# The last block's output projection made twice: three split products, and whole-precision products beside them

## The chip, the cores and the metric

The kernel runs on one core of one Trainium2 chip. The metric is the device time of one execution in microseconds (us). A core has a matrix engine (TensorE, PE in the profile, its weight loads PEld), a vector engine (VectorE, DVE), a scalar engine (ScalarE, ACT), a general engine (GpSimd, POOL) and a sync engine (SyncE, SP), which here issues nearly all DMA transfers. Each engine works through its own list of instructions in order and waits on semaphores for the others.

## What is computed

A transformer block with modulation by a condition, on 2048 rows of 512 numbers; 32 heads of 16 numbers share one key and one value head. All inputs and outputs are 32-bit floats.

```python
sa, ca, ga, sb, cb, gb = six rows of 512 from silu(c) @ w_mod
h = layernorm(x) * (1 + ca) + sa
x = x + ga * (softmax(q k' / 4) v) @ wo          # q = h @ wq, k = h @ wk, v = h @ wv
h = layernorm(x) * (1 + cb) + sb
x = x + gb * (gelu(h @ w1 + b1) @ w2 + b2)
```

The change concerns the third line for the last 256 rows alone: the output projection `@ wo`, with `ga` already multiplied into its weights.

## The kernel before, in words

**Blocks and units.** The rows go in eight blocks of 256. A block has eight attention units of four heads; the units' score products, exponentials and value products fill most of the run. What follows a block's attention (output projection, second layer norm, the two MLP layers) is a generator, `rest_steps` (L813), which hands out batches of matrix products. For blocks 0 to 6 they are woven between the attention of the next block. The last block (number 7, `fast=True`) has nothing left to be woven into; its products are issued whole, by `whole` (L181, products at L183), one after another at the end of the program.

**Split products.** A 32-bit operand is kept as two tiles of the type fp32r, a rounded one ("H") and the rest ("L"). A product is then three: H by H, H by L and L by H, added in PSUM. `batches` (L167) lists them. For the output projection, `out_pairs` (L858) gives the attention result `onH`, `onL` as the stationary operand (128 x 128) and the weights `woH`, `woL` as the moving one (128 x 512). There are four groups of 128 contraction rows (`KD` = 4) and two row tiles `t` of 128 rows, so 24 products for the block.

**The last block step by step.** Three of the four groups are projected early (18 products). The fourth waits for the last attention unit, whose sums are inverted (L691), go through DRAM (L694, L669) and scale the unit's result (L671); then it is split on ScalarE (L132) and VectorE (L137). During that wait the generator yields `TAIL[0]` = 4 ticks, and in each tick `tick` (L1473) issues a batch of what is left of block 6's second MLP layer (`w2ps`). Then the six products of the last group follow. For each row tile, VectorE adds x to the sum (`add_x`, L833), takes the statistics in two halves (`stats`, L840), joins them (`rstd`, L846 and L847), GpSimd takes the power -1/2 (L849), and VectorE makes the normalized rows `xh` (`xhat`, L852). Meanwhile `yield TAIL[1]` (L884, 8 ticks) lets block 6's last 24 `w2ps` products be issued. Then TensorE transposes `xh` (`turn2`, L917, with four filler products at L811, `stir`, after each row tile), ScalarE scales and shifts (L905), the result is split again, and the two MLP layers follow (`w1ps`, `w2ps`), with GELU on ScalarE and VectorE between them. At the end `store` (L1008) adds x1 to the sums (L1011) and sends 256 KB per row tile to DRAM (L1012).

**Pools and banks that matter.** The tile tag `ot` has two buffers that are used in turn; the output tiles of `store` live there, so a buffer is free again only when its transfer to DRAM has landed. `xh` has one buffer. `bank()` (L731) gives PSUM banks in a fixed rotation. SyncE's list has, shortly before the last projection, three transfers of 1024 KB each for MLP weights (L829), and then block 6's two output tiles (L1012), one whose sum is ready before the last projection, and one after block 6's last 24 products.

Of the kernel before, what the change touches and what calls it, by code (L numbers as in the profile page):

```python
# [8 lines left out]
F32 = mybir.dt.float32  # L9
F32R = mybir.dt.float32r  # L10
AF = mybir.ActivationFunctionType
ALU = mybir.AluOpType
AX = mybir.AxisListType

P = 128
# [30 lines left out]
def raw(ap):  # L46
    return ap.bitcast(F32)
# [3 lines left out]
def adaln_mqa_mlp(  # L51
# [15 lines left out]
    nc = tc.nc  # L67
    _, S, D = x.shape
# [3 lines left out]
    KD = D // P  # L72
# [18 lines left out]
    psum = ctx.enter_context(tc.tile_pool(name="psum", bufs=1, space=bass.MemoryType.PSUM))  # L91
# [49 lines left out]
    state = {"mods": False, "q": NB * KD, "busy": False, "turns": 1}  # L141
# [25 lines left out]
    def batches(ps, pairs, size, ready=lambda n: True, begin=True, end=True):  # L167

        todo = [(a, b_) for wh, wl, xh, xl in pairs for a, b_ in ((wh, xh), (wl, xh), (wh, xl))]
        last = len(todo) - 1  # L170

        ends = list(range(len(todo), 0, -size))[::-1]
        if ends[0] == 1:
            ends.pop(0)
        for begin_, end_ in zip([0] + ends, ends):
            part = range(begin_, end_)
            while not ready(part[-1] // 3):
                yield -1
            yield [(ps, *todo[n], begin and n == 0, end and n == last) for n in part]
# [544 lines left out]
    def rest(b, fast):  # L724
# [61 lines left out]
        ready = {}  # L786
        later(*((4, lambda: norm(0)) if fast else (2, fetch)))
        return rest_steps(b, fast, rp, bank, ons, ready)

    early = {}  # L790
# [22 lines left out]
    def rest_steps(b, fast, rp, bank, ons, ready):  # L813
# [3 lines left out]
        woH, woL = wts_pool["wo"]  # L817
        for hf in range(w // HQ):
# [5 lines left out]
            x1, w1ts = early[b]  # L824
            xh = rp.tile([P, 2, D], F32, name=f"xh2_{b}_{hf}", tag="xh2", bufs=1)
# [6 lines left out]
            def add_x(t, ps):  # L832
                nc.vector.tensor_tensor(out=x1[:, t, :], in0=ps, in1=x1[:, t, :], op=ALU.add)  # L833
# [5 lines left out]
            def stats(t, h):  # L839
                nc.vector.bn_stats(out=st[:, t, h, :], in_=x1[:, t, h * D // 2:(h + 1) * D // 2])  # L840
# [3 lines left out]
            def rstd(t0, t1):  # L844
                for t in range(t0, t1):
                    nc.vector.bn_aggr(out=mv[:, t, :], in_=st[:, t].rearrange("p h n -> p (h n)"))  # L846
                (nc.vector if fast else nc.gpsimd).tensor_scalar(out=ve[:, t0:t1], in0=mv[:, t0:t1, 1], scalar1=EPS,  # L847
                                                                 scalar2=0.0, op0=ALU.add, op1=ALU.add)
                nc.gpsimd.tensor_tensor(out=rs[:, t0:t1], in0=ve[:, t0:t1], in1=mhalf[:, t0:t1], op=ALU.pow)  # L849

            def xhat(t):
                (nc.vector if fast else nc.gpsimd).tensor_scalar(out=xh[:, t, :], in0=x1[:, t, :], scalar1=mv[:, t, 0:1],  # L852
                                                                 scalar2=rs[:, t:t + 1], op0=ALU.subtract, op1=ALU.mult)
# [4 lines left out]
            def out_pairs(t, gs):  # L858
                sl = slice(t * P, (t + 1) * P)
                return [(onH[:, g, sl], onL[:, g, sl], woH[:, g, :], woL[:, g, :]) for g in gs]  # L860

            pss = []
            for t in range(2):
                ps = psum.tile([P, D], F32, name=f"wops{b}_{hf}_{t}", **bank())
# [8 lines left out]
                    later(3 - 2 * t + 2 * h, lambda t=t, h=h: stats(t, h))  # L873
            if fast:
                yield TAIL[0]
                for t in range(2):
                    yield from batches(pss[t], out_pairs(t, [KD - 1]), BATCH, begin=False)
                    add_x(t, pss[t])
                    stats(t, 0)
                    stats(t, 1)  # L880
                    rstd(t, t + 1)
                for t in range(2):
                    xhat(t)
                yield TAIL[1]  # L884
# [45 lines left out]
            else:  # L930
                for dp in range(KD // 2):
                    ps = psum.tile([P, 2, HQ], F32, name=f"tp2_{b}_{hf}_{dp}", **bank())
# [55 lines left out]
            for f in range(GROUP if fast else 0, NF):  # L988
# [3 lines left out]
                ps = psum.tile([P, HQ], F32, name=f"w1ps{b}_{hf}_{f}", **bank())  # L992
# [27 lines left out]
            for t in range(2):  # L1020
                sl = slice(t * P, (t + 1) * P)
                for cols in (slice(0, D), ):
                    place = dict(tag="m", bufs=3) if b == len(blocks) - 2 and t else bank()
                    ps = psum.tile([P, D], F32, name=f"w2ps{b}_{hf}_{t}_{cols.start}", **place)
# [496 lines left out]
```

## Time and profile before

| what | us |
|---|---|
| median of 3 runs | 1563.27 (1562.41 to 1563.35) |
| the profiled execution | 1561.89 |
| its span (first to last instruction) | 1560.1 |
| PE busy | 1543.2 |
| DVE busy | 1400.8 |
| ACT busy | 1227.4 |
| POOL busy | 681.5 |
| granted TensorE clock | 1.0 in all slices |

The profile of one execution lists the instructions of each engine with start and duration. A line such as `L183 PE MATMUL w2ps<-w2H,gH 128*128 128x512` names the code line, the engine, the operation, the tile written and those read, the part of the array used (128 x 128) and the moving operand's shape. "Chain of work that ended last" is found by following back from the last instruction to whatever released each step. A busy TensorE is counted from records with modelled ends, so it says little about how closely products follow one another; their start times say more.

### The profile page before, as it was taken

The numbers are of one execution on the slowest core, as the hardware profiler recorded it, in microseconds if no ns is written. First come the engines' busy times: TensorE is split into PE (matmuls) and PEld (weight loads), VectorE is DVE, ScalarE is ACT, GpSimd is POOL, SyncE is SP. The second block draws the span as 40 slices with busy tenths as digits, with TensorE's granted clock in tenths as the row PEclk, the third lists the DMA queues.
The fourth block names the chain that finished last, engine by engine and source line by source line (L and its number), as shares of the span: only waits on it lengthen the run. The fifth ranks groups of instructions, "written<-read, shape, count | busy, mean of one in ns | idle before, by whom it ended". The sixth has DMA issues, their size and how long they took to land.

```text
span 1560.1 us, 41350 instructions
## 1 busy us (share of the span) xinstructions
PE 1543.2 (99%) x16347; PEld 955.2 (61%) x16347; DVE 1400.8 (90%) x2479; ACT 1227.4 (79%) x2392; POOL 681.5 (44%) x1194
## 2 busy tenths in 40 slices
PE   7999999999999999999999999999999999999999
PEld 4456555567655665557655675556655676556657
DVE  7999999999999999999999999999999999999725
ACT  5577778788878887788877887788877888778953
POOL 5545433867322570246522562245611474225721
PEclk9999999999999999999999999999999999999999
DMA  7225412312030211202012120302112120211241
GB/s 250 92 93 197 148 56 85 124 52 97 19 109 19 83 59 36 94 28 99 30 54 76 55 86 23 109 14 100 44 49 80 46 97 17 84 55 63 84 159 52
DMA packets 83125, 121.61 MB, mean 78 GB/s; under 512 B 19614, under 2 KB 56222, under 8 KB 82676
## 3 DMA queue, kind: packets, MB, share of 16 engines
q1 hardware_dynamic: 82916, 118.97, 22.9%
q8 instruction: 129, 2.11, 0.6%
q14 instruction: 64, 0.52, 0.1%
q10 hardware_dynamic: 16, 0.00, 0.0%
HBM read 91.13 MB, written 27.27 MB: 76 GB/s over the span
## 4 chain that ended last, share of the span: by engine, by line
PE 84%; DVE 10%; issue 3%; POOL 2%; DMA 1%; ACT 1%; SPq 0%; POOLq 0%; DVEq 0%
PE acc L633 28%; PE m L507 24%; PE e L612 15%; DVE mx L512 8%; PE w1ps L193 8%; PE w2ps L183 2%; PE w1ps L183 1%; DMA xt<-in_A_x_dram 1%; PE w2ps L193 1%; PE qps L193 1%; PE tp L193 1%; PE wops L193 1%; PE kps L162 1%; DVE st L840 1%; DVE x L833 1%
## 5 line engine op out<-in xcount | busy, mean ns | idle before, releaser
L512 DVE TENSOR_REDUCE mx<-m 128x1 f32<-128x512 f32 x2048 | 1269.3, 681 | 87.7 <-PE m L507 64.7
L616 ACT ACTIVATE p<-e 128x512 f32<-128x512 f32 x2048 | 1098.0, 598 | 254.8 <-PE e L612 106.4
L507 PE MATMUL m<-ks,qst 64*128 64x512 f32 x2048 | 832.9, 429 | 2.0 <-DVE mx L512 0.6
L612 PE MATMUL e<-qst,ks 64*128 64x512 f32 x2048 | 739.9, 413 | 0.0
L633 PE MATMUL acc<-p,va 128*32 128x256 f32 x8192 | 548.0, 385 | 0.0
L507 PEld LDWEIGHTS m<-ks,qst 64*128 64x128 f32 x2048 | 367.1, 184 | 211.6 <-DVE mx L512 174.0
L612 PEld LDWEIGHTS e<-qst,ks 64*128 64x128 f32 x2048 | 358.7, 185 | 92.3 <-ACT p L616 64.0
L633 PEld LDWEIGHTS acc<-p,va 128*32 128x32 f32 x8192 | 214.5, 109 | 213.7 <-issue 110.7
L555 POOL TENSOR_SCALAR mt<-turned 8x32 f32<-8x32 f32 x256 | 53.1, 208 | 419.5 <-DVE turned L561 407.4
L193 PE MATMUL w1ps<-h2H,w1t 64*128 64x256 f32 x1216 | 232.7, 287 | 0.0
L193 PEld LDWEIGHTS w1ps<-h2H,w1t 64*128 64x128 f32 x1216 | 183.6, 185 | 28.4 <-issue 14.4
L193 PE MATMUL w1ps<-h2L,w1t 64*128 64x256 f32 x608 | 167.0, 275 | 0.0
L193 PE MATMUL w2ps<-w2H,gH 64*128 64x512 f32 x264 | 115.9, 439 | 0.0
L193 PEld LDWEIGHTS w1ps<-h2L,w1t 64*128 64x128 f32 x608 | 112.8, 185 | 0.0
L193 PE MATMUL w2ps<-w2L,gH 64*128 64x512 f32 x264 | 103.4, 392 | 0.0
L193 PE MATMUL w2ps<-w2H,gL 64*128 64x512 f32 x264 | 103.0, 390 | 0.0
L959 POOL TENSOR_SCALAR tt<-tt 128x256 f32<-128x256 f32 x77 | 31.0, 403 | 143.1 <-ACT tt L958 109.8
L137 POOL TENSOR_TENSOR gL<-z,gH 128x256 fp32r<-128x256 f32 x77 | 56.9, 739 | 6.4
L960 POOL TENSOR_TENSOR tt<-tt,z 128x256 f32<-128x256 f32 x77 | 56.8, 738 | 6.4
L970 POOL TENSOR_TENSOR z<-tt,z 128x256 f32<-128x256 f32 x77 | 56.4, 733 | 6.0
L969 POOL TENSOR_TENSOR tt<-tt,z 128x256 f32<-128x256 f32 x77 | 56.5, 734 | 0.0
L193 PE MATMUL wops<-woH,onH 64*128 64x512 f32 x112 | 49.8, 444 | 0.0
(190 smaller groups left out, 1495.3 us busy)
## 6 DMA issues: line engine op xcount, KB each, us to landing
w1t<-dw SPq DMA_DIRECT2D x82, 512.0 KB
qst<-dq SPq DMA_DIRECT2D x384, 32.0 KB
do<-oc SPq DMA_DIRECT2D x64, 128.0 KB
dw<-w1s SPq DMA_DIRECT2D x11, 512.0 KB
xt<-in_A_x_dram SPq DMA_DIRECT2D x4, 1024.0 KB
dq<-qH SPq DMA_DIRECT2D x16, 256.0 KB
dq<-qL SPq DMA_DIRECT2D x16, 256.0 KB
x<-in_A_x_dram SPq DMA_DIRECT2D x8, 512.0 KB
```

Source lines behind the costliest of these rows:

```text
L137: eng_l.tensor_tensor(out=dst_l, in0=src, in1=raw(dst_h), op=ALU.subtract)
L183: nc.tensor.matmul(ps, a, b_, start=first_, stop=last_)
L193: ins = nc.tensor.matmul(ps, a[rows], b_[rows], start=first_ and s == 0, stop=last_ and s == 1)
L507: nc.tensor.matmul(m, qsts[u][rows, j, t * P:(t + 1) * P], ks[rows, kc * 512:(kc + 1) * 512], start=True, stop=True)
L512: nc.vector.tensor_reduce(out=self.mx[u][:, i, kc:kc + 1], in_=m, axis=AX.X, op=ALU.max)
L555: nc.gpsimd.tensor_scalar(out=mt[:, g:g + 32], in0=turned[g:g + 4 * T, :], scalar1=1.0, scalar2=0.0, op0=ALU.mult, op1=ALU.add)
L612: nc.tensor.matmul(e, ks[rows, kt * P:(kt + 1) * P], rhs, start=True, stop=True)
L616: ins = nc.scalar.activation(dst, e, AF.Exp, scale=0.25)
L633: ins = nc.tensor.matmul(accs[u][32 * cidx:32 * cidx + 32, :], va[:, kt, :], rhs, start=kt == 0, stop=kt == NKT - 1)
L960: nc.gpsimd.tensor_tensor(out=tt, in0=tt, in1=z, op=ALU.mult)
L969: nc.gpsimd.tensor_tensor(out=tt, in0=tt, in1=z, op=ALU.mult)
L970: nc.gpsimd.tensor_tensor(out=z, in0=tt, in1=z, op=ALU.add)
```

## The change

In the last block, after each row tile's sum is finished and added to x1, the sum is also copied to an `ot` tile (`cp0`, `cp1`). Then the same projection is made once more without splitting: for each group, GpSimd adds `woH` and `woL` into one half of `xh`, and TensorE multiplies the unsplit attention result `os` (type F32) by it, for both row tiles, into two further PSUM tiles (`full0`, `full1`). VectorE subtracts the copied sum from the new one, and adds 2048 times the difference to x1, ahead of the statistics. So the value of x1 for these rows is changed by 2048 times the rounding difference of the two ways of making the product. In the order of instructions the eight new products stand on TensorE behind the last six `wops` products and ahead of block 6's last 24 `w2ps` products. The four additions stand on GpSimd behind the splitting of the first three groups and ahead of the power. On VectorE the two copies stand behind the two additions of x1, and `cp1` waits for a DMA: it takes the buffer of block 6's first output tile.

```diff
             if fast:
                 yield TAIL[0]
+                cps = []
                 for t in range(2):
                     yield from batches(pss[t], out_pairs(t, [KD - 1]), BATCH, begin=False)
                     add_x(t, pss[t])
+                    cp = rp.tile([P, D], F32, name=f"cp{t}", tag="ot", bufs=2)
+                    nc.vector.tensor_copy(out=cp, in_=pss[t])
+                    cps.append(cp)
+                fulls = [psum.tile([P, D], F32, name=f"full{t}", **bank()) for t in range(2)]
+                for g in range(KD):
+                    nc.gpsimd.tensor_tensor(out=xh[:, g % 2, :], in0=raw(woH[:, g, :]), in1=raw(woL[:, g, :]), op=ALU.add)
+                    yield [(fulls[t], state["os"][:, 0, g, t * P:(t + 1) * P], xh[:, g % 2, :], g == 0, g == KD - 1) for t in range(2)]
+                for t in range(2):
+                    ps = fulls[t]
+                    nc.vector.tensor_tensor(out=cps[t], in0=ps, in1=cps[t], op=ALU.subtract)
+                    nc.vector.scalar_tensor_tensor(out=x1[:, t, :], in0=cps[t], scalar=2048.0, in1=x1[:, t, :], op0=ALU.mult, op1=ALU.add)
                     stats(t, 0)
                     stats(t, 1)
                     rstd(t, t + 1)
                 for t in range(2):
                     xhat(t)
                 yield TAIL[1]
```

## The prediction

> **What bounds the kernel now.** The page comes first, for the share of each engine.
>
> ```profile
> span 1560.1 us, 41350 instructions
> PE 1543.2 (99%) x16347; PEld 955.2 (61%) x16347; DVE 1400.8 (90%) x2479; ACT 1227.4 (79%) x2392; POOL 681.5 (44%) x1194
> PE 84%; DVE 10%; issue 3%; POOL 2%; DMA 1%; ACT 1%; SPq 0%; POOLq 0%; DVEq 0%
> ```
>
> TensorE carries 84% of the chain that ended last. That is an average over the run, and the change touches only the last 50 us, so the second view is the chain inside the window from 1500 us on, in order of time (start, duration, what).
>
> ```profile
> 1514.40 0.41 ACT onH L132
> 1514.81 0.04 issue
> 1514.85 1.89 PE wops L183 x6
> 1516.74 5.51 PE w2ps L183 x24
> 1522.25 0.44 PE tp L917 x4
> 1522.68 0.92 PE stir L811 x4
> 1523.61 0.44 PE tp L917 x4
> 1524.04 0.93 PE stir L811 x4
> 1524.98 15.31 PE w1ps L183 x132
> 1540.29 15.95 PE w2ps L183 x66
> 1556.24 0.04 DVEq L1011
> 1556.27 0.04 issue
> 1556.32 0.69 DVE ot L1011
> ```
>
> From 1514.85 to 1556.24 every piece is TensorE. The last six projection products, block 6's 24 `w2ps`, the transposes and both MLP layers stand one behind the other without a piece of another engine between them. So time added to TensorE's list here is added to the end, and a wait put into it as well.
>
> The third view is the timeline of this stretch. It tells how much cover the layer norm on VectorE has.
>
> ```profile
> 1516.08 0.69 DVE L833 TENSOR_TENSOR x<-wops,x 128x512 f32<-128x512 f32 x1 [0.82 <-PE wops L183]
> 1516.34 0.40 PE L183 MATMUL wops<-woL,onH 128*128 128x512 f32 x1
> 1516.58 0.39 PE L183 MATMUL w2ps<-w2H,gH 128*128 128x512 f32 x1
> 1517.90 0.68 DVE L833 TENSOR_TENSOR x<-wops,x 128x512 f32<-128x512 f32 x1
> 1519.72 0.54 DVE L852 TENSOR_SCALAR xh<-x,mv,rs 128x512 f32<-128x512 f32 x1
> 1520.72 0.55 DVE L852 TENSOR_SCALAR xh<-x,mv,rs 128x512 f32<-128x512 f32 x1 [0.45 <-POOL rs L849]
> 1522.09 0.60 PE L917 MATMUL tp<-ident,xh 128*128 128x128 f32 x4
> ```
>
> VectorE's chain from the first addition of x to the first finished `xh` half runs from 1516.08 to 1520.26, that is 4.18 us. The 24 products issue from 1516.58 until the transposes at 1522.09, 5.51 us or 0.23 us each. `xh` is finished 1.83 us before TensorE comes to it: that is all the cover there is.
>
> **The change part by part. First, the eight products.** Their operands have the plain type F32. No F32 product of 128 stationary columns is in the trace, but narrower ones are. The rows are groups by line and shape (busy, mean ns), the third one a burst in the timeline.
>
> ```profile
> L292 PE MATMUL modl<-wml,csb 128*32 128x512 f32 x32 | 4.3, 605 | 0.0
> L183 PE MATMUL w2ps<-w2L,gH 128*128 128x512 f32 x44 | 17.8, 404 | 0.0
> 65.36 1.07 PE L292 MATMUL modl<-wml,csb 128*32 128x512 f32 x8
> L917 PEld LDWEIGHTS tp<-ident,xh 128*128 128x128 f32 x8 | 1.0, 140 | 0.3
> ```
>
> The code asks for 16 `modl` products and the trace has 32 instructions: an F32 product becomes two, one behind the other. One of these lasts 605 ns where an fp32r product of the same 512 columns lasts 404, so it holds the array some 0.20 us longer than the 0.23 us at which fp32r products follow one another: 0.43 us. The burst says the same: eight instructions are four products side by side in four column strips of 32, so two instructions in turn on each; 1.07 us less the 0.16 by which a record (0.39) outlasts its slot (0.23) leaves 0.91, 0.455 each. I take 0.455 and expect that 128 columns instead of 32 change nothing, as the array works on all strips at once. Sixteen instructions are **7.3 us** (6.9 at 0.43). Ends for the unknown: 3.7 us, were each of the 16 as short as an fp32r product, and 10.2 us, were the weight load (taken as 0.188, the 0.19 of the loads in this stretch) in line with each (16 x 0.64). The transposes are the nearest F32 case with full loads: four pass in 0.44 us, 0.11 each, while one load lasts 140 ns, so the loads lie beside the work, and the low end of that span holds.
>
> The page "TensorE: Matmul & The Clock Gate" of the Trainium skill (Part 3, The mechanism) states that "LDWEIGHTS overlaps with in-flight MATMULs only when row_grp differs". The new products all use the full rows, so by that rule their sum would be 10.2 us. By the rows it is 7.3, and the trace does not agree with the rule for full rows: `w2ps` products of 128 x 128 follow one another in 0.23 us.
>
> **Second, the additions on GpSimd.** Rows: the last split of the early groups, the same form of operation, and the power (idle time before it in brackets).
>
> ```profile
> 1488.96 0.74 POOL L137 TENSOR_TENSOR onL<-os_last,onH 128x256 fp32r<-128x256 f32 x1
> L856 POOL TENSOR_TENSOR x<-x,b2g 128x512 f32<-128x512 f32 x16 | 20.2, 1287 | 0.0
> 1518.06 0.57 POOL L849 TENSOR_TENSOR rs<-ve,mhalf 128x1 f32<-128x1 f32 x1 [28.37 <-DVE ve L847]
> ```
>
> GpSimd idles 28 us from 1489.70. The first two additions run there, done by 1492.3, long before TensorE asks at 1516.6. The third must wait until both products of group 0 have read its half of `xh`: 1516.57 + 4 x 0.455 = 1518.4; with 1.29 us it is done at 1519.75, and TensorE, busy with group 1 until 1520.2, does not wait. The fourth starts at 1520.25 and is done at 1521.6, ahead of 1522.0, when group 2 ends. Cost zero; the cover is 0.4 us. Were an addition 0.5 us slower, TensorE would stand 0.1 us, once or twice.
>
> **Third, VectorE's list.** Two copies, two subtractions and two multiply-adds of 128 x 512 are added ahead of the statistics.
>
> ```profile
> L458 DVE COPY q<-qps 128x512 f32<-128x512 f32 x11 | 7.6, 690 | 0.0
> L952 DVE SCALAR_TENSOR_TENSOR tt<-tt,z 128x256 f32<-128x256 f32 x11 | 4.6, 420 | 4.3 <-ACT tt L951 4.3
> ```
>
> A copy out of PSUM takes 0.69. A subtraction with PSUM is L833's form, 0.69. The multiply-add exists at half the size, 0.42; at 512 it lies between 0.42 and 0.84, and I take 0.68, as L833's two-operand form. From the start of the first subtraction to the first finished `xh` half it is the old 4.18 us, with the subtraction in the place of the addition, plus two multiply-adds with their gaps: 4.18 + 2 x 0.71 = **5.60 us**.
>
> When can it start? `full0` ends with the 14th of the 16 instructions, as its last product stands before `full1`'s: 14 slots from 1516.57 are 1522.94, with 0.16 to drain 1523.1. But `cp1` stands ahead in VectorE's list and waits for block 6's first output tile to land. The issue, the DMA in stretches of half a microsecond (last two columns: share of the DMA engines, GB/s), and from the chain the shortest wait of VectorE for a DMA:
>
> ```profile
> 1513.37 9.99 SPq L1012 DMA_DIRECT2D out_dram<-ot  x2
> ...
> 1521.00:1521.50 0.50, 0.50 (x4) 0.42 (x3) 0.27 (x1) 0.00 (x0) 0.00 (x0) 1.00 0.95 344
> 1521.50:1522.00 0.50, 0.50 (x4) 0.41 (x3) 0.00 (x0) 0.00 (x0) 0.00 (x0) 1.00 0.10 37
> 1522.00:1522.50 0.50, 0.50 (x7) 0.41 (x4) 0.21 (x1) 0.00 (x0) 0.00 (x0) 1.00 0.06 25
> 1522.50:1523.00 0.50, 0.50 (x5) 0.42 (x4) 0.48 (x1) 0.00 (x0) 0.00 (x0) 1.00 0.04 16
> 1523.00:1523.50 0.50, 0.50 (x4) 0.36 (x3) 0.00 (x0) 0.00 (x0) 0.00 (x0) 1.00 0.00 0
> ...
> 1510.39 3.42 DMA os_last<-dr
> 1513.94 0.44 DVE os_last L671
> ```
>
> The tile is issued at 1513.37, but behind three weight transfers of 1024 KB, and the engines are full until 1521.5. A thin tail follows, as of one engine that is late; the last packets move before 1523.0, then nothing. I put the landing at 1523.3, between 1522.2 (without the late engine) and 1524. VectorE starts 0.13 us after a landing (1513.81 to 1513.94), so `cp1` runs from 1523.45 to 1524.14, and the first subtraction starts at 1524.17, a microsecond after `full0` is there. With 5.60 us the first `xh` half is done at 1529.77, and TensorE has it at 1529.8.
>
> **The sum.** On TensorE alone: 1516.58 + 7.28 + 5.51 = 1529.37 for the first transpose, against 1522.09: +7.3 us. Over VectorE: 1529.8, +7.7 us. The later one decides, so TensorE stands some 0.4 us ahead of the transposes. The second half follows 1.0 us after the first, and TensorE asks for it 1.36 us after it began (0.44 of transposes and 0.92 of filler), so it adds nothing. Block 6's second output sum, which VectorE takes behind `xh`, is done at 1531.5, before ScalarE's results come (1524.46 before, 1532.2 after). Everything later waits for TensorE and shifts as a whole; the freed output buffer at the end was free anyway. So the profiled execution of 1561.89 us (span 1560.1) becomes 1569.6. It lies 1.4 us under the median of the runs; the median becomes 1563.27 + 7.7 = **1571.0 us**.
>
> **The rivals.** *The landing is early (TensorE alone decides).* If the late engine of the tail is chance, the tile lands near 1522.2, `cp1` is done by 1523.0, and VectorE is ready at 1528.8; then +7.3, 1570.6 us. The tail in one execution speaks neither way. *The landing is late.* At 1524.5 every later step of the VectorE sum moves by 1.2: +8.9, 1572.2 us. The empty stretch after 1523.0 speaks against it. *The weight loads stand in line.* The sixteen take 10.2 us: 1516.58 + 10.2 + 5.51 = 1532.3, with VectorE ready at 1531.4; +10.2, 1573.5 us. The transposes speak against it. *The array is twice as quick* (3.7 us): the landing still sets the end, since `cp1` does not depend on the products, so +7.7 stays with a landing at 1523.3. *Not slower.* TensorE's work after the projection would have to hold slack for all that is added: waits inside the 31.3 us of `w1ps` and `w2ps` for weight pieces or GELU results, hidden by modelled ends, which a later start would spare. It decides from 4.6 us of such slack on (7.7 less the 3.1 that can be told), and would give 1563.3 to 1566.4 us. But what those products wait for (GELU) itself starts from the transposes and shifts with them, and the three weight pieces had landed by 1523. That the products are not issued can be excluded: they stand in TensorE's list.
>
> **How the numbers follow.** Forecast (landing sets it, +7.4 to +8.0) 0.57; early landing 0.26; late landing 0.07; loads in line 0.07; not slower 0.03. 0.2% of this time, 3.1 us, is about what a measurement of this kernel can tell from no change. Slower by more: 0.97; within it 0.02; faster 0.01. The range runs from a landing at 1522.2 with the products at 0.43 (+6.9), less 0.9 for the spread of the runs before, to the loads in line (+10.2): 1569.3 to 1573.5 us.
>
> **What would show it.** In the changed profile: 16 `full` instructions with starts 0.43 to 0.46 us apart and no idle time on POOL's account; `cp1` idle until a DMA, some 5 us, starting near 1523.4; the first subtraction near 1524.2, not 1523.1; the transposes 7.7 us later than 1522.09 with some 0.4 us of idle TensorE before them, released by VectorE's `xh`; all later pieces of the chain of the same length. I am wrong if the starts of the `full` instructions are 0.6 us apart, if `cp1` starts without waiting, or if `w1ps` and `w2ps` of the last block take another time than 15.3 and 16.0 us.

## The result, and the profile after

| | before | after |
|---|---|---|
| median, us | 1563.27 (1562.41 to 1565.77, 5 runs) | 1569.47 (1568.84 to 1570.0, 5 runs) |
| ratio to before | | 1.0038, 95% interval 1.0024 to 1.0053 |
| profiled execution, us | 1561.89 | 1568.84 |
| span, us | 1560.1 | 1567.1 |
| PE / DVE / POOL busy, us | 1543.2 / 1400.8 / 681.5 | 1549.7 / 1404.5 / 688.7 |

The change makes the kernel 6.2 us slower by the medians; the interval of the ratio, times 1563, is 3.8 to 8.3 us. The two profiled executions differ by 7.0 us.

The chain that ended last, after, in the window from 1500 us on (start, duration, what):

```profile
1514.91 1.89 PE wops L183 x6
1516.80 6.89 PE full L183 x16
1523.69 5.52 PE w2ps L183 x24
1529.20 0.44 PE tp L929 x4
1529.64 0.92 PE stir L811 x4
1530.56 0.44 PE tp L929 x4
1531.00 0.93 PE stir L811 x4
1531.93 15.32 PE w1ps L183 x132
1547.26 15.97 PE w2ps L183 x66
1563.30 0.69 DVE ot L1023
```

Against the chain before there is one new piece, `full`, 6.89 us. All others have their old lengths, and none of another engine has come between them. That is the whole difference, 6.9 of 7.0 us. The rest of the story stands in the timeline of the same stretch, after (idle time before an instruction and what ended it in brackets):

```profile
1516.13 0.69 DVE L833 TENSOR_TENSOR x<-wops,x 128x512 f32<-128x512 f32 x1 [0.82 <-PE wops L183]
1516.64 7.05 PE L183 MATMUL full<-xh,os_last 128*128 128x512 f32 x16
1518.67 1.27 POOL L885 TENSOR_TENSOR xh<-woH,woL 128x512 f32<-128x512 f32 x1 [26.76 <-PE full L183]
1520.38 1.26 POOL L885 TENSOR_TENSOR xh<-woH,woL 128x512 f32<-128x512 f32 x1 [0.45 <-PE full L183]
1522.45 0.69 DVE L881 COPY cp<-wops 128x512 f32<-128x512 f32 x1 [4.43 <-DMA out_dram<-ot]
1523.06 0.68 DVE L889 TENSOR_TENSOR cp<-full,cp 128x512 f32<-128x512 f32 x1
1528.14 0.54 DVE L852 TENSOR_SCALAR xh<-x,mv,rs 128x512 f32<-128x512 f32 x1
1529.04 0.60 PE L929 MATMUL tp<-ident,xh 128*128 128x128 f32 x4
1529.14 0.55 DVE L852 TENSOR_SCALAR xh<-x,mv,rs 128x512 f32<-128x512 f32 x1 [0.46 <-POOL rs L849]
```

The wait of the second copy for block 6's output tile is there, 4.43 us long, but it ends at 1522.45. The first half of `xh` is done at 1528.68, 0.36 us before TensorE is through with the 24 products and starts the transposes at 1529.04. So VectorE's path stays hidden, by little.

### The profile page after: what moved, and what is told of

Same layout as the page of the kernel before. It is cut to its first block, busy times and chain, and to the rows that moved or that the text cites. A ratio compares the mean times of both kernels' runs of the same rounds, so it can differ in the third digit from the quotient of the medians.

```text
span 1567.1 us, 41394 instructions
## 1 busy us (share of the span) xinstructions
PE 1549.7 (99%) x16363; PEld 956.2 (61%) x16363; DVE 1404.5 (90%) x2485; ACT 1228.1 (78%) x2392; POOL 688.7 (44%) x1198
## 4 chain that ended last, share of the span: by engine, by line
PE 87%; DVE 10%; DMA 2%; ACT 1%; issue 0%; POOL 0%; SPq 0%; ACTq 0%; DVEq 0%
PE acc L633 30%; PE m L507 25%; PE e L612 16%; DVE mx L512 8%; PE w1ps L193 8%; PE w2ps L183 2%; PE w2ps L193 2%; PE qps L193 1%; PE w1ps L183 1%; DMA xt<-in_A_x_dram 1%; PE tp L193 1%; PE kps L162 1%; PE wops L193 1%; DVE st L840 1%; DVE x L833 1%; PE full L183 0%
```

## The experiments

What comes before the last projection differs between executions by a microsecond or more, and it stands ahead of what was edited in all runs but two (the later landing, and two groups ahead of the wait). So the profiles are compared by the time from the start of L671 (the scaling of the last unit's result, which all the rest waits for) to the end of the span: 1560.1 - 1513.94 = 46.16 us before and 1567.1 - 1514.00 = 53.10 after, +6.94. This is called the *tail* below. The start of L671 in each run is in the table at the end of this section. Each tail is that of one execution; the three runs in which TensorE's list decides and is the same (the change, the products alone, the change with copies that wait for no transfer) agree within 0.08 us.

**Products without VectorE's part.**

```diff
-                    cp = rp.tile([P, D], F32, name=f"cp{t}", tag="ot", bufs=2)
-                    nc.vector.tensor_copy(out=cp, in_=pss[t])
-                    cps.append(cp)
...
-                    ps = fulls[t]
-                    nc.vector.tensor_tensor(out=cps[t], in0=ps, in1=cps[t], op=ALU.subtract)
-                    nc.vector.scalar_tensor_tensor(out=x1[:, t, :], in0=cps[t], scalar=2048.0, in1=x1[:, t, :], op0=ALU.mult, op1=ALU.add)
```

> The change without VectorE's part: copies, subtractions and multiply-adds are left out, so the unsplit sums are made and not used and x1 is that of before. Theory (TensorE's 16 new instructions set the end): the transposes stand 6.9 us later than before, span +6.9, as with the whole change. Rival (VectorE's added work or its wait carries part of the +6.9): the span comes out visibly below +6.9, by the part that VectorE carried.

Measured: ratio 1.0048 (1.0031 to 1.0064); tail +6.99, the `full` piece 6.88 us. Taking VectorE's six instructions and the wait away changes nothing.

**The change with copies that wait for no transfer.**

```diff
-                    cp = rp.tile([P, D], F32, name=f"cp{t}", tag="ot", bufs=2)
+                    cp = rp.tile([P, D], F32, name=f"cp{t}", tag="wf", bufs=3)
```

> The whole change, with the copies in a buffer that waits for no transfer. Theory (TensorE's path is the later one when the tile lands at 1522.4): the same as the change, span +6.9, the wait costs nothing. Rival (the wait still costs something inside the change, as predicted, 0.4 us): +6.5.

Measured: 1.0043 (1.0028 to 1.0058); tail +6.91. In the profiled execution of the change the wait costs nothing.

**VectorE's part without products.** The loop over `g` is left out, and the subtraction reads the split sum.

```diff
-                fulls = [psum.tile([P, D], F32, name=f"full{t}", **bank()) for t in range(2)]
-                for g in range(KD):
-                    nc.gpsimd.tensor_tensor(out=xh[:, g % 2, :], in0=raw(woH[:, g, :]), in1=raw(woL[:, g, :]), op=ALU.add)
-                    yield [(fulls[t], state["os"][:, 0, g, t * P:(t + 1) * P], xh[:, g % 2, :], g == 0, g == KD - 1) for t in range(2)]
...
-                    ps = fulls[t]
+                    ps = pss[t]
```

> The change without the four additions on GpSimd and without the eight products; the subtraction takes the split sum itself, so 2048 times zero is added. Theory (the end is the later of two paths, and the path over the landing of block 6's output tile was only 0.4 us shorter than TensorE's): the copy still waits for the landing at about 1522.4, first xh half at 1528.7, span +6.6 although no product is left. Rival A (only VectorE's extra work counts): +2.2. Rival B (TensorE alone): 0.

Measured: 1.0059 (1.0044 to 1.0074); tail +9.34. With all added products gone the kernel is not faster than the change but, in the profiles, 2.4 us slower. The chain of this run:

```profile
1513.23 10.07 DMA out_dram<-ot
1523.30 0.02 issue
1523.32 0.69 DVE cp L881
...
1529.10 0.46 DVE xh L852
1529.57 0.05 issue
1529.61 1.11 PE tp L925 x4
1530.72 1.71 PE stir L811 x4
1532.43 0.85 PE tp L925 x4
1533.28 1.28 PE stir L811 x4
1534.56 14.97 PE w1ps L183 x132
```

The landing has become part of the chain, as the theory says. From L671 to the transposes it is 1529.61 - 1514.20 = 15.41 us, against 1522.25 - 1513.94 = 8.31 before: +7.1 (0.5 more than expected, as the tile landed later than in the change's run). But the transposes and their fillers take 4.95 us instead of 2.73, and the expectation did not have that. The busy times in stretches of this run tell why (PE is the second number, the granted clock the third from the right):

```profile
1522.00:1524.00 2.00, 0.49 (x3) 0.06 (x1) 0.68 (x2) 0.00 (x0) 0.00 (x0) 1.00 0.03 10
1524.00:1526.00 2.00, 0.00 (x0) 0.00 (x0) 1.93 (x5) 0.00 (x0) 0.00 (x0) 1.00 0.00 0
1526.00:1528.00 2.00, 0.00 (x0) 0.00 (x0) 1.86 (x6) 0.00 (x0) 0.57 (x1) 0.77 0.00 0
1528.00:1530.00 2.00, 0.39 (x2) 0.39 (x3) 1.49 (x5) 0.00 (x0) 0.79 (x1) 0.50 0.00 0
1530.00:1532.00 2.00, 2.00 (x8) 1.71 (x7) 1.15 (x2) 0.00 (x0) 0.00 (x0) 0.50 0.00 0
1532.00:1534.00 2.00, 2.00 (x9) 1.61 (x8) 0.47 (x2) 1.02 (x2) 0.00 (x0) 0.52 0.34 131
1534.00:1536.00 2.00, 2.00 (x18) 1.91 (x17) 1.43 (x5) 1.13 (x2) 0.73 (x1) 1.00 0.00 0
```

TensorE has nothing to do from 1522.5 on; its clock is halved while it idles and stays at 0.50 for the transposes and the fillers, until about 1534.

**The same, with copies that wait for no transfer.** Both edits above.

> As the run without products, but the copies go to a buffer that waits for no transfer (tag wf instead of ot). Theory: the wait is gone, VectorE runs on and the first xh half comes at about 1524.2, 2.1 us behind the 24 products that cover it: span +2.2. Rival (the wait is for something else than the tile's landing): still near +6.6.

Measured: 1.0020 (1.0011 to 1.0030); tail +3.88, where +2.2 was expected. The transposes start 10.22 us after L671, +1.9, so the wait was indeed for the tile. Of the other 2.0 us, 0.4 is a later start of the last output tile (told below), and some 1.6 are the clock again: TensorE had idled for only 1.92 us.

```profile
1525.58 1.08 PE L925 MATMUL tp<-ident,xh 128*128 128x128 f32 x4 [1.92 <-DVE xh L852]
1526.00:1528.00 2.00, 2.00 (x8) 1.67 (x7) 1.13 (x2) 0.00 (x0) 0.00 (x0) 0.50 0.00 0
```

The profiled execution is the slowest of ten, 1567.23 us against a median of 1565.71, and the mean clock of the ten lies between 0.998 and 1.0. So it is not shown that the clock fell in all of them.

**Filler products in the idle stretch.** To the run without products:

```diff
             if fast:
+                stir([4 * i for i in range(28)])
                 tps = [psum.tile([P, 2, HQ], F32, name=f"tp2_{b}_{hf}_{dp}", **bank()) for dp in range(KD // 2)]
```

> The run without products again (copies wait for the output tile's landing), with 28 filler products of 128 x 512 ahead of the transposes, whose results nobody reads. They fill 6.4 us of the 7.1 us in which TensorE stood idle. Theory (the +9.3 of that run is 7.1 of waiting and 2.2 of transposes and fillers at half clock, because TensorE had idled): the granted clock stays 1.00, transposes to first MLP product take 2.7 us again instead of 5.0, span about +7 although more work is issued. Rival (the slow transposes have another cause, such as their operands): still 5.0 us and +9.3.

Measured: 1.0052 (1.0036 to 1.0069); tail +7.67. The granted clock is 1.00 in every stretch. Transposes to first MLP product take 1532.70 - 1529.75 = 2.95 us, of which 0.2 is the first group, which starts from rest:

```profile
1523.46 0.69 DVE cp L881
...
1529.75 0.66 PE tp L925 x4
1530.41 0.92 PE stir L811 x4
1531.33 0.44 PE tp L925 x4
1531.77 0.93 PE stir L811 x4
1532.70 15.32 PE w1ps L183 x132
```

With 28 more products the tail is 1.7 us shorter. So 2.0 of the 2.2 us were the clock, and the idling brought it down. (`w1ps` behind the slow transposes had taken 14.97 us instead of 15.32, so the whole costs less than 2.0.) The two medians' intervals overlap; the profiles carry this verdict. In the three runs without products the last output tile starts some 0.4 us later behind its products than in the others; what causes that stays open.

**Two groups instead of four.** The mark of each sum's last product moves with the loop.

```diff
-                for g in range(KD):
+                for g in range(2):
```

> The change with the unsplit products of two of the four groups only (half the sum, so what is added to x1 is another number). Theory (later of two paths): TensorE would be ready after +3.45, but the copy waits for the landing and the first xh half comes at 1528.7: span +6.6, nearly nothing saved. Rival (TensorE's list alone sets the time): +3.45.

Measured: 1.0053 (1.0038 to 1.0068); tail +9.89. In the profiles, half the products cost more than all of them; the intervals of the two ratios overlap. The copy started at 1524.54, 9.59 us after L671, later than in the change's run (8.45); TensorE idled 4.12 us ahead of the transposes and then ran them at half clock:

```profile
1530.82 1.12 PE L929 MATMUL tp<-ident,xh 128*128 128x128 f32 x4 [4.12 <-DVE xh L852]
```

From L671 to the transposes: 15.87 us, +7.56; the other 2.3 us come with the half clock. TensorE's list alone would give +3.45, so that rival has fallen.

**All products twice.** The marks of each sum's first and last product move with the loop.

```diff
-                for g in range(KD):
+                for n in range(2 * KD):
+                    g = n % KD
```

> The change with all unsplit products made twice into the same sums (so twice the sum, and another number is added to x1). Theory: 32 instructions at 0.431 us, span +13.8; VectorE's chain starts later with the products and stays 0.4 us ahead. Rival (weight loads or GpSimd's additions stall the longer series): above +14.5.

Measured: 1.0082 (1.0066 to 1.0097); tail +13.85, as expected. The chain's piece:

```profile
1517.01 13.79 PE full L183 x32
```

13.79 / 32 = 0.431 us an instruction, the same as 6.89 / 16. Six additions on GpSimd stand between the products, and no stall shows.

**A later landing.** One transfer of 1 MB, from DRAM to DRAM, is put behind the weight transfers on their queue.

```diff
+                nc.sync.dma_start(out=spare, in_=dw1[0:2])
...
+    spare = tc.dram_tile([2, P, 2, KD, P], F32, name="spare")
```

> The whole change, and one more transfer of 1 MB between two places in DRAM, queued behind the weight transfers and ahead of block 6's output tile. Theory (later of two paths): the tile lands some 2.6 us later, near 1525; the transposes start 6.3 us after the landing, near 1531.3, span about +9.2, with idle TensorE ahead of the transposes. Rival (TensorE's list alone): +6.9, the landing has no effect.

Measured: 1.0050 (1.0033 to 1.0067); tail +8.54 (expected +9.2; the extra transfer delayed the landing by 2.1 us instead of 2.6). The chain goes over the landing now, and the transposes start 6.3 us after it:

```profile
1513.75 11.59 DMA out_dram<-ot
1525.34 0.02 issue
1525.36 0.04 DVE cp L882
...
1531.65 0.66 PE tp L930 x4
```

TensorE idled 1.66 us here, and the clock stayed at 1.00.

**Products behind block 6's 24 products.** Copies in `wf`, and:

```diff
+                yield TAIL[0]
                 fulls = [psum.tile([P, D], F32, name=f"full{t}", **bank()) for t in range(2)]
```

> The whole change, copies in a buffer that waits for no transfer, and the unsplit products moved behind block 6's 24 products instead of ahead of them; the same work on every engine. Theory (the 24 products are the cover of VectorE's chain): the subtraction starts at 1528.3, the first xh half comes at 1534.0, TensorE idles 4.9 us ahead of the transposes, span +11.9. Rival (only the sum of TensorE's work counts): +6.9.

Measured: 1.0089 (1.0074 to 1.0104); tail +14.28, where +11.9 was expected. The order of the same work is worth 7.4 us of tail against the change with the free tile: 4.87 us of idling ahead of the transposes, as expected, and about 2.5 more at half clock (transposes and fillers took 5.4 us instead of 2.7; the profile gives 1.12, 1.71, 0.85 and 1.71). This execution is 3.4 us longer than the next of its run; 6.8 us at half clock near its start, ahead of the tail, would make that much (last section).

**Two groups ahead of the wait.** Copies in `wf`; the loop over `g` is cut into `range(2)` ahead of `yield TAIL[0]` and `range(2, KD)` at its old place.

> The whole change, copies in a buffer that waits for no transfer, and the unsplit products of groups 0 and 1 issued ahead of the wait for the last attention unit instead of behind it; the same work. Theory (the only TensorE time that the change could have for nothing is the idle stretch ahead of the last six split products, 0.55 us): span +6.4, the last six products 2.9 us later than before. Rival (that stretch is not usable, or VectorE then sets the end): +6.9 or more.

Measured: 1.0038 (1.0023 to 1.0053). VectorE's list has L671 behind block 6's sum here, so the tail is taken from L691: 59.5 us, against 60.7 for the change with the free tile, 60.6 for the change and 53.2 before. The wait for the last unit has left the chain:

```profile
1510.54 3.43 PE full L183 x8
1513.97 3.91 PE w2ps L183 x17
1517.88 1.40 PE wops L183 x6
1519.29 3.43 PE full L183 x8
```

It is the shortest whole change here, by about a microsecond in the profile (the intervals of the ratios overlap), and still 6.2 us longer than before: no other idle stretch of TensorE is left there to fill.

| run | start of L671 | span | tail against before | copy starts after L671 |
|---|---|---|---|---|
| before | 1513.94 | 1560.1 | | |
| the change | 1514.00 | 1567.1 | +6.94 | 8.45 |
| products only | 1514.05 | 1567.2 | +6.99 | |
| no products | 1514.20 | 1569.7 | +9.34 | 9.12 |
| no products, free tile | 1515.36 | 1565.4 | +3.88 | 3.95 |
| change, free tile | 1514.63 | 1567.7 | +6.91 | 3.96 |
| two groups | 1514.95 | 1571.0 | +9.89 | 9.59 |
| twice | 1514.19 | 1574.2 | +13.85 | 8.30 |
| landing late | 1514.80 | 1569.5 | +8.54 | 10.56 |
| behind the 24 | 1517.96 | 1578.4 | +14.28 | 3.95 |
| no products, filled | 1514.37 | 1568.2 | +7.67 | 9.09 |

## Why the prediction was right or wrong, point by point

- *Direction and place*: right. Everything from the projection to the end is TensorE, and what is added there is added to the end.
- *The eight products*: the mechanism was right, two instructions each, one behind the other, with the weight loads beside them (load 189 ns, slot 431 ns), but the size was off. The step that took 0.455 us from the burst failed: 0.431 was measured, the 0.43 that the first row gave. The sum is 6.89 us instead of 7.28. All of the burst's 1.07 us, less the drain, was put down to the two instructions in turn; in its trace the four strips start one behind the other, 0.02 us in all, and the first instruction of each lasts 617 ns where the second lasts 592. These two make up the 0.05 us by which two slots came out too long. That the loads stand in line has fallen in all runs with `full`; the sentence of the Trainium skill on it (page "TensorE: Matmul & The Clock Gate", Part 3, The mechanism) does not hold for these rows.
- *GpSimd's additions*: right in the cost, 1.27 and 1.26 us and no gap to speak of between the `full` instructions, also in the doubled run. The cover was smaller than the 0.4 us predicted: the third addition was to start as soon as the four slots ahead of it had passed, at 1518.36 here (1516.64 + 4 x 0.43), and started at 1518.67. It is done at 1519.94, some 0.1 us ahead of its group's first slot.
- *VectorE's list*: right. From the first subtraction to the first `xh` half it is 5.62 us; 5.60 was the estimate. The multiply-add took 0.69.
- *Which path ends last*: wrong for the profiled execution, and this is the step that the forecast of +7.7 hangs on, since VectorE's path does not contain the products' size. The landing was put at 1523.3, and the copy started at 1522.45, so the case named "the landing is early" (0.26) came true and TensorE alone decided, with 6.89 us. There was no 0.4 us of idle TensorE ahead of the transposes. Had it landed where it was put, the second path would have ended last by some 0.6 us (a copy 9.3 us after L671, and 6.29 from there to the transposes, against the 15.04 of TensorE's list).
- *That the landing can decide*: shown. In the runs without products, filled, two groups and late landing the transposes start 6.3 us after the copy's start. In the change TensorE is ready 15.04 us after L671, so a copy that starts later than about 8.75 us after L671 costs time. In the runs that do not touch the transfers it started after 8.30, 8.45, 9.09, 9.12 and 9.59. If that spread is chance, some executions of the change should pay 0.3 to 0.8 us more than the profiled one; this is worked out, not seen. The five are one profile each, and the three late ones are of kernels with fewer products, so that the spread is chance is not shown either.
- *The early-landing rival's price*, +7.3, was too high by the same 0.4 us of the products. At 0.431 it is +6.9, and the tail shows +6.94.
- *The late-landing rival and the bounds* had no clock in them. In the four runs whose TensorE idled for 1.9 us or more ahead of the transposes, the wait had a second price of 1.6 to 2.5 us. That did not touch the change itself, whose TensorE never idles there.

The medians' +6.2 lies under the profiles' +6.9, inside its interval; the runs of before alone spread over 3.4 us.

## What to carry to other kernels

Where two paths end within half a microsecond of each other, price both, and look for what varies from run to run in one of them: here the landing of a transfer that a reused buffer waits for. Taking work from the longer path then gains nothing, as the runs without products and with two groups show, until the wait is gone as well. And an idle matrix engine can cost more than the idle time: here from 1.92 us of idling on. Put the cost of the lower clock for what follows into every rival that makes it wait.

## What the runs showed of the hardware that was not expected

- The granted clock of TensorE falls to 0.50 in or behind idle stretches of 1.92, 4.12, 4.87 and 7.12 us, and did not in one of 1.66 us. The fall comes while it idles or just after: in the run with 7.12 us between 1526 and 1528, some 4 to 5 us after the last product, in the one with 1.92 us after about 2. It lasts 3.4 us after the stretch of 1.92 and 6.8 us after the three longer ones; transposes and fillers took 4.6 to 5.4 us instead of 2.7. The Trainium skill, page "TensorE: Matmul & The Clock Gate" (Part 1, What's actually happening), has the half rate after at least one idle window of about 3.4 us; 1.92 us were enough here, so the idle length from which a fall can come is shorter than that figure.
- A long idle stretch isn't the only way to a fall. In the run with the products behind the 24, the clock stood at 0.50 from about 62 to 68.8 us (the third number from the right), and in the 2 us ahead of it the records show TensorE idle for 0.28 us only. The runs of the change and of before have as little idling there (0.26 and 0.28 us) and no fall. What decides it stays open. 6.8 us at half clock lose 3.4 us, about what L671 starts later in that run than in the others (1517.96 against 1513.94 to 1515.36).

```profile
60.00:62.00 2.00, 1.72 (x6) 0.75 (x6) 1.88 (x4) 1.23 (x3) 0.00 (x0) 0.99 0.00 0
62.00:64.00 2.00, 2.00 (x4) 1.01 (x4) 1.66 (x3) 0.03 (x1) 0.00 (x0) 0.50 0.00 0
```

- An F32 product of 128 x 128 by 512 columns is two instructions of 0.431 us, 0.86 us in all; three fp32r products, the split form, are 3 x 0.23 = 0.69 us.
- On VectorE an instruction can start before the one ahead has ended. `cp1` at 1522.45 lasts 0.69 us, and the first subtraction, which does not use it, starts at 1523.06, after 0.61. The multiply-add, which uses the subtraction's result, starts 0.71 after it, behind its end at 0.68.
